# Attention into two expert layers on one core: k and v of two batches loaded as six tokens on 96 partitions, loads ordered apart from their use, half of the sums of squares on VectorE

## The chip, the cores and the metric

The kernel runs on one core of one Trainium2 chip. The metric is the device time of one execution in microseconds (us), lower is better. The kernel before takes 1116.54 us (median of 3 runs, 1115.36 to 1117.87).

## The reference, cut to what matters

All inputs are float32 but for the weights `moe_w1`, `moe_w2`, `moe_w3` and `moe_w_out`, which are float64. `q`, `k` and `v` have the shape (4 batches, 8 heads, 576 tokens, 64).

```
kv  = einsum('bhsd,bhse->bhde', k, v)            # per head: 64 x 64
out = einsum('bhsd,bhde->bhse', q, kv)
rms = sqrt(mean(out*out, axis=-1) + 1e-6)
x   = (out / rms * g_norm), as 2304 tokens x 512
h   = ((x @ moe_w1) * (x @ moe_w2)) @ moe_w3      # d_ff = 1024
y   = h @ moe_w_out                               # 2304 x 512
p   = probs / (sum(probs) + 1e-9)                 # 4 experts
result = sum over e of p[:, e] * (relu(y @ w1[e]) @ w2[e])
```

## The kernel before, in words

**Three stretches.** The attention and the first layer make up the "front" (about the first third of the time). Then three groups of 768 tokens go through the four experts. All large products are done as three matmuls each on parts of the numbers (`mm3`, lines 321 to 325: high x high, high x low, low x high), and many of them in a Winograd-like form with seven products in place of eight. These matmuls on lines 323 to 325 fill TensorE for most of the time.

**The attention, in units.** `unit(b, p)` (line 689) computes two heads of one batch. It loads q, k and v for the first 512 of the 576 tokens, with four tokens on each of 128 partitions (`head_pair`, line 554): 128 x 2 x 256 numbers, 256 KB, in rows of 1 KB. The last 64 tokens of k and v of all eight heads come once for a batch by `rest_kv` (line 563): the tile `kvr`, 64 x 8 x 64 numbers, 128 KB for k and 128 KB for v, in rows of 256 B. On TensorE a unit then has five steps: `outer` (line 713; 8 matmuls of 64 x 64 on `kv` and 2 on `kvr`, into a bank that is copied to `kvb`), the transposes of q (`qs`, line 684, copied to `qt`), `inner` (line 741; `kvb` times `qt`), and, after the norm, the transposes of `x` (line 684). The last 64 tokens of q of two batches together are a `rest_unit` (line 751).

**The norm** (`normed_turned`, line 575). The sum of squares of each head over 64 columns is made in one of two ways. With `summing`, ScalarE squares each of the eight heads by an instruction of its own that also adds up (line 592, 8 ACTIVATEs with an accumulator read behind each). Without, ScalarE squares the whole bank by one instruction (line 588), and VectorE adds up (line 598). In the kernel before, `SUMMING = 18` makes all 18 do it the first way. GpSimd then takes the root (lines 604 and 605), and VectorE scales (line 608). After the transposes, ScalarE or VectorE writes `xr` (line 626) and splits it into `xth` and `xtl` (lines 368 and 373).

**Weights.** `decode` (line 445) loads 512 KB of float64 as `w1raw`, `w2raw`, `woraw` or `w3raw`, and turns them to float32 on ScalarE and VectorE (lines 460 to 494).

**What sets the order.** The program is a list of operations with the engines on which each can run. `FRONT` (line 35) is a list of parts written out by hand; each part is a stage. The planner (`Plan.order`, line 139) walks through time with a cost for each operation, gives each free engine the ready operation of the earliest stage, and writes the instructions in that order. It holds a count of tiles: `RINGS` allows 9 tiles of `attention` (q, k, v) at a time. A load is an operation like the others, queued in its unit's stage. All loads and stores go through one queue, SP's. Eight transfers are under way at a time: the ninth waits until the first has landed, and the two small loads of `g_norm`, which ScalarE issues (line 424), take two of these eight places once. Where TensorE has little to do at the start, `FILL` and `WARM` add matmuls on an identity (lines 420 and 1693), whose results are not used.

Of the kernel before, what the change touches and what calls it, by code (L numbers as in the profile page):

```python
# [13 lines left out]
I64 = mybir.dt.int64  # L14
# [4 lines left out]
P = 128  # L19
RAWS = 5  # L20
TILES = 99
BANKS = 8
RINGS = {"attention": 9, "decoded": 12}
WINDOW = 14
AHEAD = 3
LATER = 6
PLAIN = 1
SUMMING = 18
WARM = 10
# [5 lines left out]
FRONT = (  # L35
# [12 lines left out]
)  # L48
# [210 lines left out]
def attention_moe_kernel(  # L259
# [57 lines left out]
    def half(name, dt=F32, ring=None):  # L317
        return Buf("h", name, [P, 512], dt, ring)
# [23 lines left out]
    def load(buf, *parts, key=None, queue="sp", cost=None):  # L342
        def emit(_):
            for dst, src in parts:
                (nc.sync if queue == "sp" else nc.scalar).dma_start(
                    out=dst(buf.tile), in_=src[:, :] if isinstance(src, Buf) else src
                )

        add(
            {queue: cost or (1.48 if buf.kind == "r" else 0.68)}, emit,  # L350
            reads=[src for _, src in parts if isinstance(src, Buf)], writes=[(buf, key)], latency=2.6,
        )
# [91 lines left out]

    def decode(name, src, shape=None):

# [3 lines left out]

        raw = Buf("r", name + "raw", [P, 512], I64)
        load(raw, ((lambda t: t.rearrange("p (k f) -> p k f", k=KD)) if shape else whole, src))
        val, add_ = half("val", ring="decoded"), half("add", I32, "decoded")
# [118 lines left out]

    summed = []

    def normed_turned(ps, places, whole_values=None):

# [4 lines left out]
        ss = Buf("n", "ss", [P, 8, 1], F32)  # L581

        summing = SUMMING > len(summed)
        summed.append(t)

# [78 lines left out]
    def zeroed(name):  # L664
        t = half(name)
        add({"pool": 0.5}, lambda _: nc.gpsimd.memset(t.tile, 0.0), writes=[t])
        return t
# [20 lines left out]

    def unit(b, p):
        first = b not in kvb  # L690
        if first:
            kvb[b] = zeroed("kvb")
        loaded = []
        for name, src in (("q", q), ("kv", k), ("kv", v)):
            raw = half(name, ring="attention")
            load(raw, (heads, head_pair(src, b, p)), cost=0.82)
            loaded.append(raw)
        qraw, ks, vs = loaded
        if first:
            rest_kv(b)  # L700
        kr, vr = kvr[b]
        ps = bank()

        def outer(e):
# [9 lines left out]

        add({"pe": 0.9}, outer, reads=[ks, vs, kr, vr], writes=[ps])
        for i in range(2):
# [28 lines left out]
        if b == B - 1 and p < HP // 2:  # L745
            normed_turned(po, [], xr[b, p])
        else:
            xt[b, p] = Pair("xt")
            normed_turned(po, [(512, xt[b, p], whole, whole, None)], xr[b, p])

    def rest_unit(g):
        qraw = half("q", ring="attention")
# [26 lines left out]
        if g == 0:  # L779
# [8 lines left out]
            for i in range(2)  # L788
        ])

# [73 lines left out]
    pair_w = {}  # L864
    weights = {}

    def pair_weights(g, n, i):
# [37 lines left out]
        return made  # L905

    def weight(n, f):

        if (n, f) not in weights:
            weights[n, f] = decode(f"w{n + 1}", columns((moe_w1, moe_w2)[n], f), True)  # L910
        return weights[n, f]
# [725 lines left out]
    def expert_shares():  # L1637
# [4 lines left out]
        fn.__name__: fn for fn in (  # L1642
            bilinear_pair, bilinear_plain, expert_shares, mixed, mixed_product,
            norm_scale, rest_unit, row, unit, w3o_summed,
# [33 lines left out]

    for stage, (fn, args) in enumerate(items):
        plan.stage = stage  # L1680
        fn(*args)

    with tc.manual_schedule():
# [42 lines left out]
```

## Time and profile before

| | |
|---|---|
| runs | 1116.54 us median of 3 (1115.36 to 1117.87) |
| profiled execution | 1117.49 us, span 1115.7 us |
| mean granted TensorE clock | 0.998 of full speed |
| TensorE (PE) busy | 1103.3 us, 99% of the span |
| VectorE (DVE) busy | 810.5 us, 73% |
| ScalarE (ACT) busy | 600.6 us, 54% |
| GpSimd (POOL) busy | 47.1 us, 4% |
| DMA | 272.91 MB, 72.5% of the queues' time by SP's queue |

The profiled execution's own time is 1.8 us more than its span (the time from the first to the last instruction), and 0.95 us above the median of the runs. Matmuls are pipelined: one is shown as longer than the distance to the next, so a busy share of 99% alone does not tell how much of it is useful. The trace shows float32 matmuls as two records each (`x8` for the four of line 741).

### The profile page before, as it was taken

The numbers are of one execution on the slowest core, as the hardware profiler recorded it, in microseconds if no ns is written. First come the engines' busy times: TensorE is split into PE (matmuls) and PEld (weight loads), VectorE is DVE, ScalarE is ACT, GpSimd is POOL, SyncE is SP. The second block draws the span as 40 slices with busy tenths as digits, with TensorE's granted clock in tenths as the row PEclk, the third lists the DMA queues.
The fourth block names the chain that finished last, engine by engine and source line by source line (L and its number), as shares of the span: only waits on it lengthen the run. The fifth ranks groups of instructions, "written<-read, shape, count | busy, mean of one in ns | idle before, by whom it ended". The sixth has DMA issues, their size and how long they took to land.

```text
span 1115.7 us, 19375 instructions
## 1 busy us (share of the span) xinstructions
PE 1103.3 (99%) x6856; PEld 1022.3 (92%) x6856; DVE 810.5 (73%) x1656; ACT 600.6 (54%) x1472; POOL 47.1 (4%) x57
## 2 busy tenths in 40 slices
PE   7999999999999999999999999999999999999998
PEld 7888888888888999889999999999999999999998
DVE  4888888889879898788667745547588646474684
ACT  6998754556636655545444455434455445444540
POOL 4513200000000000000000000000000000000000
PEclk9999999999999999999999999999999999999999
DMA  9999993450330599999977935778679867685846
GB/s 272 288 336 329 380 370 102 137 167 20 95 95 29 171 349 351 345 365 327 339 262 239 363 126 198 259 247 288 217 256 328 282 239 259 238 299 195 280 140 203
DMA packets 173697, 272.91 MB, mean 245 GB/s; under 512 B 21792, under 2 KB 89376, under 8 KB 173600
## 3 DMA queue, kind: packets, MB, share of 16 engines
q1 hardware_dynamic: 173440, 271.68, 72.5%
q8 instruction: 54, 0.88, 0.3%
q14 instruction: 43, 0.35, 0.1%
q10 hardware_dynamic: 160, 0.00, 0.0%
HBM read 188.78 MB, written 82.84 MB: 243 GB/s over the span
## 4 chain that ended last, share of the span: by engine, by line
PE 95%; ACT 2%; DMA 1%; DVE 1%; issue 0%; POOL 0%; DVEq 0%; ACTq 0%
PE b L323 30%; PE b L325 30%; PE b L324 30%; PE b L684 2%; PE b L741 1%; PE b L713 1%; DMA q<-in_q_dram 0%; ACT x L592 0%; ACT hth L368 0%; DMA w1raw<-in_moe_w_dram 0%; DMA woraw<-in_moe_w_out_dram 0%; PE b L776 0%; DVE s L1501 0%; DVE acc L1576 0%; ACT qs L729 0%
## 5 line engine op out<-in xcount | busy, mean ns | idle before, releaser
L672 ACT COPY u<-b 128x384 f32<-128x384 f32 (+1 forms) x191 | 96.5, 505 | 194.5 <-PE b L325 189.7
L325 PE MATMUL b<-w,htl 128*128 128x256 f32 x672 | 189.9, 283 | 0.0
L324 PE MATMUL b<-w,hth 128*128 128x256 f32 x672 | 189.8, 282 | 0.0
L323 PE MATMUL b<-w,hth 128*128 128x256 f32 x672 | 189.6, 282 | 0.0
L1401 DVE TENSOR_TENSOR u<-u,b 128x384 f32<-128x384 f32 x144 | 79.5, 552 | 124.2 <-PE b L325 66.9
L1576 DVE SCALAR_TENSOR_TENSOR acc<-b,pn,acc 128x256 f32<-128x256 f32 x144 | 68.7, 481 | 85.1 <-PE b L325 84.9
L325 PEld LDWEIGHTS b<-w,htl 128*128 128x128 f32 x672 | 128.4, 191 | 0.0
L323 PEld LDWEIGHTS b<-w,hth 128*128 128x128 f32 x672 | 128.0, 191 | 0.2
L324 PEld LDWEIGHTS b<-w,hth 128*128 128x128 f32 x672 | 128.1, 191 | 0.0
L368 ACT CAST hth<-s 128x384 fp32r<-128x384 f32 x128 | 62.9, 512 | 51.1 <-DVE s L1501 48.0
L1412 ACT ACTIVATE u<-u 128x384 f32<-128x384 f32 x96 | 50.5, 526 | 62.0 <-DVE u L1401 61.9
L325 PE MATMUL b<-wdh,htl 128*128 128x512 f32 x192 | 75.5, 393 | 0.0
L324 PE MATMUL b<-wdl,hth 128*128 128x512 f32 x192 | 75.4, 393 | 0.0
L323 PE MATMUL b<-wdh,hth 128*128 128x512 f32 x192 | 74.7, 389 | 0.0
L373 DVE TENSOR_TENSOR htl<-s,hth 128x384 fp32r<-128x384 f32 x128 | 67.3, 550 | 3.5 <-ACT hth L368 3.5
L373 DVE TENSOR_TENSOR htl<-u,hth 128x384 fp32r<-128x384 f32 x96 | 49.9, 551 | 5.8 <-ACT hth L368 5.8
L368 ACT CAST hth<-u 128x384 fp32r<-128x384 f32 x96 | 46.3, 510 | 0.4
L323 PE MATMUL b<-th,weh 128*128 128x512 f32 x112 | 44.5, 397 | 0.4 <-ACT u L672 0.4
L325 PE MATMUL b<-th,wel 128*128 128x512 f32 x112 | 43.7, 390 | 0.0
L324 PE MATMUL b<-tl,weh 128*128 128x512 f32 x112 | 43.7, 390 | 0.0
L325 PEld LDWEIGHTS b<-wdh,htl 128*128 128x128 f32 x192 | 36.0, 188 | 7.6
L324 PEld LDWEIGHTS b<-wdl,hth 128*128 128x128 f32 x192 | 36.0, 188 | 5.9
(291 smaller groups left out, 3037.8 us busy)
## 6 DMA issues: line engine op xcount, KB each, us to landing
we<-we SPq DMA_DIRECT2D x240, 256.0 KB, 5.3
w<-w2kept SPq DMA_DIRECT2D x112, 512.0 KB, 4.5
we<-weh SPq DMA_DIRECT2D x48, 256.0 KB, 3.8
we<-wel SPq DMA_DIRECT2D x48, 256.0 KB, 3.7
w3raw<-in_moe_w_dram SPq DMA_DIRECT2D x16, 512.0 KB, 3.7
e1raw<-in_moe_w_dram SPq DMA_DIRECT2D x32, 256.0 KB, 4.4
e2raw<-in_moe_w_dram SPq DMA_DIRECT2D x32, 256.0 KB, 4.4
w2kept<-wth SPq DMA_DIRECT2D x32, 256.0 KB, 3.8
```

What stands on the lines that cost most here:

```text
L323: nc.tensor.matmul(ps, w[0], x[0], start=first, stop=False, skip_group_check=more)
L324: nc.tensor.matmul(ps, w[0], x[1], start=False, stop=False, skip_group_check=more)
L325: nc.tensor.matmul(ps, w[1], x[0], start=False, stop=last, skip_group_check=more)
L368: nc.scalar.copy(to(dst.high.tile), value(src.tile))
L373: nc.vector.tensor_tensor(out=to(dst.low.tile), in0=value(src.tile), in1=to(dst.high.tile), op=ALU.subtract)
L672: lambda e: nc.scalar.copy(to(dst.tile), value(src.tile)) if e == "act"
L684: nc.tensor.transpose(ps[:, c], raw[:, c], ident)
L713: nc.tensor.matmul(ps[c, c], a, b_, start=r == 0, stop=r == R)
L741: nc.tensor.matmul(po[:, c], qt[:, c], kvb[b][:, p * P:(p + 1) * P], start=True, stop=True)
L1401: lambda _: nc.vector.tensor_tensor(out=t[:, :W], in0=base[:, :W], in1=ps[:, :W], op=ALU.add),
L1412: lambda eng: nc.scalar.activation(out=t[:, :W], in_=src[:, :W], func=ACTF.Relu)
L1576: nc.vector.scalar_tensor_tensor(out=a[:, to], in0=ps[:, c], scalar=sc, in1=a[:, to], op0=ALU.mult, op1=ALU.add)
```

## The change

**Loads of k and v.** For batches 0 and 1 (`SIXES`) k and v of a unit are loaded head by head: all 576 tokens as six on each of 96 partitions, four loads of 96 x 384 numbers (144 KB, rows of 1.5 KB) in place of two of 256 KB. `outer_sixes` has 12 matmuls of 64 x 64 on 96 rows in place of 10. The `kvr` tiles of these two batches, their loads and their zeroing on GpSimd fall away. Batches 2 and 3 are as before.

**Loads as parts.** `fetch` and `fetch_weight` are parts of `FRONT` of their own, ahead of the unit or weight that uses them, and don't count as a stage. `FRONT` is a new list, the ring of attention tiles is 12 in place of 9.

**Sums of squares.** Each unit has a third number, `summing`. Nine of 18 have 1 (ScalarE adds up, as before); nine have 0 (one square of 128x512 on ScalarE, the sum on VectorE).

```diff
-RINGS = {"attention": 9, "decoded": 12}
+RINGS = {"attention": 12, "decoded": 12}
...
+SIXES = (0, 1)
 PLAIN = 1
-SUMMING = 18
...
 FRONT = (
...
+    "norm_scale, fetch 1 2, fetch_weight 1 4, fetch_weight 0 7, unit 1 2 0, fetch 1 3, weight 1 4, "
+    "fetch_weight 1 0, fetch 1 1, weight 0 7, fetch 1 0, unit 1 3 0, unit 1 0 0, fetch 0 0, fetch 0 1, "
+    "fetch 0 2, fetch_weight 0 3, fetch 0 3, unit 1 1 0, unit 0 0 0, unit 0 1 1, unit 0 2 1, weight 1 0, "
+    "fetch 3 1, unit 0 3 0, bilinear_plain 0 0, rest_unit 0 1, unit 3 1 0, fetch 2 0, weight 0 3, unit 2 "
+    "2 1, unit 2 0 1, bilinear_plain 1 0, bilinear_pair 0 3, unit 2 1 1, bilinear_pair 0 2, unit 3 2 0, "
+    "unit 3 0 0, unit 3 3 1, bilinear_pair 0 1, unit 2 3 1, rest_unit 1 1, bilinear_pair 1 2, "
...
-    def normed_turned(ps, places, whole_values=None):
+    def normed_turned(ps, places, whole_values=None, summing=0):
...
+    def fetch(b, p):
+        loaded = fetched[b, p] = []
         for name, src in (("q", q), ("kv", k), ("kv", v)):
+            if b in SIXES and name == "kv":
+                for h in range(2):
+                    raw = half(name, ring="attention")
+                    load(raw, (
+                        lambda t: t[0:96, 0:6 * D].rearrange("p (r d) -> p r d", r=6),
+                        src[b, 2 * p + h].rearrange("(p r) d -> p r d", r=6),
+                    ), cost=0.45)
+                    loaded.append(raw)
+                continue
             raw = half(name, ring="attention")
             load(raw, (heads, head_pair(src, b, p)), cost=0.82)
             loaded.append(raw)
...
+            def outer_sixes(e):
+                for r in range(6):
+                    for h in range(2):
+                        c, m = slice(h * D, (h + 1) * D), slice(r * D, (r + 1) * D)
+                        nc.tensor.matmul(
+                            ps[c, c], kvs[h][0:96, m], kvs[2 + h][0:96, m], start=r == 0, stop=r == 5
+                        )
...
+    def fetch_weight(n, f):
+        weights_raw[n, f] = fetch_raw(f"w{n + 1}", columns((moe_w1, moe_w2)[n], f), True)
...
-    for stage, (fn, args) in enumerate(items):
-        plan.stage = stage
+    for fn, args in items:
         fn(*args)
+        plan.stage += fn not in (fetch, fetch_weight)
```

What this does to the order of the instructions is shown for three engines. The first is SP, the queue of the loads, from the first instruction of the program. Before:

```order
L345 DMA w1raw<-in_moe_w_dram 128x4x128
L345 DMA q<-in_q_dram 128x2x256
L345 DMA kv<-in_k_dram 128x2x256
L345 DMA kv<-in_v_dram 128x2x256
L345 DMA kvr<-in_k_dram 64x8x64
L345 DMA kvr<-in_v_dram 64x8x64
L345 DMA q<-in_q_dram 128x2x256
L345 DMA kv<-in_k_dram 128x2x256
L345 DMA kv<-in_v_dram 128x2x256
```

The same place of SP's queue now (line 346 is line 345 of the kernel before):

```order
L346 DMA q<-in_q_dram 128x2x256
L346 DMA kv<-in_k_dram 96x384 x2
L346 DMA kv<-in_v_dram 96x384 x2
L346 DMA w2raw<-in_moe_w_dram 128x4x128
L346 DMA w1raw<-in_moe_w_dram 128x4x128
L346 DMA q<-in_q_dram 128x2x256
L346 DMA kv<-in_k_dram 96x384 x2
L346 DMA kv<-in_v_dram 96x384 x2
L346 DMA w2raw<-in_moe_w_dram 128x4x128
```

The first unit's q, k and v stand ahead of all weights, and no load of `kvr` stands between the first eight units any more; up to the eighth unit there are four loads of weights (three before).

The second is TensorE (PE) around the first matmul of the bilinear layer (`xth`, `wh`; lines 323 to 325), behind the eighth unit's `outer`. Before:

```order
L684 MATMUL b<-ident,x 128x128 x4
L741 MATMUL b<-kvb,qt 128x128 x4
L713 MATMUL b<-kv 64x64 x8
L713 MATMUL b<-kvr 64x64 x2
L741 MATMUL b<-kvb,qt 128x128 x4
L684 MATMUL b<-ident,qs 128x128 x4
L323 MATMUL b<-xth,wh 128x512
L324 MATMUL b<-xtl,wh 128x512
L325 MATMUL b<-xth,wl 128x512
```

The same place now (722 is `outer_sixes`, 771 is `inner`, 324 to 326 is `mm3`):

```order
L684 MATMUL b<-ident,x 128x128 x4
L771 MATMUL b<-kvb,qt 128x128 x4
L722 MATMUL b<-kv 64x64 x12
L771 MATMUL b<-kvb,qt 128x128 x4
L684 MATMUL b<-ident,qs 128x128 x4
L324 MATMUL b<-xth,wh 128x512
L325 MATMUL b<-xtl,wh 128x512
L326 MATMUL b<-xth,wl 128x512
```

In both programs TensorE has done the same steps of units ahead of this matmul: eight times `outer`, seven times `inner`, eight transposes of q and four of `x`; each `outer` now has 12 matmuls in place of 10, and 12 fill matmuls stand among them in place of 20.

The third is ScalarE (ACT), from the first unit's copy of `qs`. Before:

```order
L729 COPY qs<-q 128x2x4x64
L672 COPY qt<-b 128x512
L368 CAST weh<-val 128x512
L729 COPY qs<-q 128x2x4x64
L672 COPY kvb<-b 64x64 x2
L672 COPY qt<-b 128x512
L592 ACTIVATE x,ss<-b 128x64 x8
L672 COPY kvb<-b 64x64 x2
```

The same place of ScalarE now:

```order
L759 COPY qs<-q 128x2x4x64
L672 COPY qt<-b 128x512
L672 COPY kvb<-b 64x64 x2
L465 ACTIVATE val<-w2raw 128x512
L474 ACTIVATE add<-w2raw 128x512
L465 ACTIVATE val<-w1raw 128x512
L588 ACTIVATE x<-b 128x512
L759 COPY qs<-q 128x2x4x64
```

The first unit's eight squares with sums (line 592) are one square of the whole bank (line 588); the sum is a TENSOR_REDUCE on VectorE (line 598).

## Rows read from the trace of the kernel before

**Rows 1.** The page's part 1: busy us (share of the span) and instructions of each engine.

```profile
PE 1103.3 (99%) x6856; PEld 1022.3 (92%) x6856; DVE 810.5 (73%) x1656; ACT 600.6 (54%) x1472; POOL 47.1 (4%) x57
```

**Rows 2.** Waits of PE from 37.3 us on: us in total, times, longest.

```profile
PE b L323 <- ACT u L672: 1.3, 5, 0.4
```

**Rows 3.** Chain of waits that ended last: start us, us, what.

```profile
15.10 1.35 PE b L741 x8
16.47 1.75 ACT x L592 x16
...
39.34 0.73 PE b L713 x20
...
43.44 0.44 PE b L684 x4
46.64 0.89 PE b L741 x8
```

**Rows 4.** Timeline of PE: start us, us, instruction [idle before <- releaser].

```profile
8.56 0.69 PE L713 MATMUL b<-kv 128*64 128x64 f32 x16 [0.90 <-DMA kv<-in_v_dram]
10.80 0.34 PE L713 MATMUL b<-kvr 128*64 128x64 f32 x4 [1.55 <-DMA kvr<-in_v_dram]
...
37.27 0.48 PE L323 MATMUL b<-xth,wh 128*128 128x512 f32 x1
...
38.05 0.40 PE L323 MATMUL b<-xth,wh 128*128 128x512 f32 x1
38.28 0.39 PE L324 MATMUL b<-xtl,wh 128*128 128x512 f32 x1
```

**Rows 5.** Stretches: length, busy us by engine, granted PE clock, DMA share, GB/s.

```profile
0.00:10.00 10.00, 7.01 (x52) 6.71 (x52) 0.96 (x4) 3.81 (x6) 6.73 (x19) 1.00 0.84 203
10.00:18.00 8.00, 6.27 (x54) 5.86 (x54) 4.85 (x9) 3.57 (x21) 0.00 (x0) 0.79 1.09 348
...
20.00:22.00 2.00, 2.00 (x32) 1.80 (x30) 1.51 (x4) 1.98 (x18) 0.39 (x1) 1.00 1.25 248
22.00:24.00 2.00, 1.40 (x26) 1.15 (x25) 1.33 (x2) 1.95 (x7) 1.72 (x2) 1.00 1.15 191
```

**Rows 6.** Timeline of SP's queue: start us, us, the load that is issued.

```profile
0.72 0.46 SPq L345 DMA_DIRECT2D w1raw<-in_moe_w_dram  x1
1.24 0.49 SPq L345 DMA_DIRECT2D q<-in_q_dram  x1
...
2.80 0.75 SPq L345 DMA_DIRECT2D kvr<-in_k_dram  x1
...
7.20 0.37 SPq L345 DMA_DIRECT2D kv<-in_k_dram  x1
...
15.74 0.37 SPq L345 DMA_DIRECT2D kv<-in_k_dram  x1
...
29.55 0.37 SPq L345 DMA_DIRECT2D kv<-in_v_dram  x1
```

**Rows 7.** Waits of all engines up to 37.3 us: the one of `g_norm`.

```profile
DVE g L425 <- DMA graw<-in_g_norm_dram: 9.0, 1, 9.0
```

**Rows 8.** Groups of ACT up to 45 us: xcount | busy us, mean ns | idle before.

```profile
L592 ACT ACTIVATE x<-b 128x64 f32<-128x64 f32 x64 | 13.3, 248 | 2.2 <-PE b L741 2.2
...
L729 ACT COPY qs<-q 128x512 f32<-128x512 f32 x6 | 3.7, 617 | 0.0
...
L672 ACT COPY qt<-b 128x512 f32<-128x512 f32 x5 | 3.0, 597 | 1.7 <-PE b L684 1.6
```

**Rows 9.** Groups of DVE up to 45 us, columns as in rows 8.

```profile
L608 DVE TENSOR_TENSOR x<-b,ss 128x512 f32<-128x512 f32 x7 | 4.8, 692 | 2.1 <-POOL ss L605 1.9
...
L474 DVE TENSOR_SCALAR val<-val 128x512 f32<-128x512 f32 x3 | 1.3, 421 | 0.0
```

**Rows 10.** Stretches, columns as in rows 5: a dip of the clock, a later stretch.

```profile
12.00:16.00 4.00, 3.29 (x16) 3.29 (x17) 2.35 (x5) 1.55 (x5) 0.00 (x0) 0.57 1.09 348
...
75.00:150.00 75.00, 75.00 (x462) 63.44 (x461) 66.88 (x126) 60.41 (x208) 14.99 (x14) 1.00 1.02 356
```

More of the change, by code (lines that the diff above doesn't have):

```diff
@@ L442, in shares, with fetch_raw, decode @@
         nc.vector.tensor_tensor(out=pn, in0=praw, in1=prec.to_broadcast([P, NT // P, NE]), op=ALU.mult)
-    def decode(name, src, shape=None):
+    def fetch_raw(name, src, shape):
         raw = Buf("r", name + "raw", [P, 512], I64)
         load(raw, ((lambda t: t.rearrange("p (k f) -> p k f", k=KD)) if shape else whole, src))
+        return raw
+    def decode(name, src, shape=None, raw=None):
+        raw = fetch_raw(name, src, shape) if raw is None else raw
         val, add_ = half("val", ring="decoded"), half("add", I32, "decoded")
@@ L571, in rest_kv @@
             )
-    summed = []
-    def normed_turned(ps, places, whole_values=None):
+    def normed_turned(ps, places, whole_values=None, summing=0):
         t = half("x")
         ss = Buf("n", "ss", [P, 8, 1], F32)
-        summing = SUMMING > len(summed)
-        summed.append(t)
         def square(e):
@@ L687, in turned @@
         return ps
[L689 to L693, printed above, removed]
-        for name, src in (("q", q), ("kv", k), ("kv", v)):
+    fetched = {}
+    def fetch(b, p):
+        loaded = fetched[b, p] = []
+        for name, src in (("q", q), ("kv", k), ("kv", v)):
+            if b in SIXES and name == "kv":
[7 more added lines that the diff above has]
+                continue
             raw = half(name, ring="attention")
@@ L697, in unit @@
             loaded.append(raw)
[L698 to L701, printed above, removed]
-        ps = bank()
+    def unit(b, p, summing=0):
+        if b not in kvb:
+            kvb[b] = zeroed("kvb")
+        sixes = b in SIXES
+        if (b, p) not in fetched:
+            fetch(b, p)
+        loaded = fetched[b, p]
+        ps = bank()
+        if sixes:
+            qraw, *kvs = loaded
+            def outer_sixes(e):
[5 more added lines that the diff above has]
+                        )
+            add({"pe": 1.08}, outer_sixes, reads=kvs, writes=[ps])
+        else:
+            qraw, ks, vs = loaded
+            if b not in kvr:
+                rest_kv(b)
+            kr, vr = kvr[b]
         def outer(e):
@@ L713, in outer @@
                     nc.tensor.matmul(ps[c, c], a, b_, start=r == 0, stop=r == R)
-        add({"pe": 0.9}, outer, reads=[ks, vs, kr, vr], writes=[ps])
+        if not sixes:
+            add({"pe": 0.9}, outer, reads=[ks, vs, kr, vr], writes=[ps])
         for i in range(2):
@@ L745, in unit, with rest_unit @@
         if b == B - 1 and p < HP // 2:
-            normed_turned(po, [], xr[b, p])
+            normed_turned(po, [], xr[b, p], summing)
         else:
             xt[b, p] = Pair("xt")
-            normed_turned(po, [(512, xt[b, p], whole, whole, None)], xr[b, p])
-    def rest_unit(g):
+            normed_turned(po, [(512, xt[b, p], whole, whole, None)], xr[b, p], summing)
+    def rest_unit(g, summing=0):
         qraw = half("q", ring="attention")
@@ L788, in rest_unit @@
             for i in range(2)
-        ])
+        ], summing=summing)
     def x_of(xs, b, kk):
@@ L865, in attention_moe_kernel @@
     weights = {}
+    weights_raw = {}
     def pair_weights(g, n, i):
@@ L905, in pair_weights @@
         return made
+    def fetch_weight(n, f):
+        weights_raw[n, f] = fetch_raw(f"w{n + 1}", columns((moe_w1, moe_w2)[n], f), True)
     def weight(n, f):
         if (n, f) not in weights:
-            weights[n, f] = decode(f"w{n + 1}", columns((moe_w1, moe_w2)[n], f), True)
+            if (n, f) not in weights_raw:
+                fetch_weight(n, f)
+            weights[n, f] = decode(f"w{n + 1}", None, True, weights_raw[n, f])
         return weights[n, f]
@@ L1642, in attention_moe_kernel @@
         fn.__name__: fn for fn in (
-            bilinear_pair, bilinear_plain, expert_shares, mixed, mixed_product,
+            bilinear_pair, bilinear_plain, expert_shares, fetch, fetch_weight, mixed, mixed_product,
             norm_scale, rest_unit, row, unit, w3o_summed,
```

19 rows, old and new, of the table FRONT are left out of this document.

## The prediction

> **What bounds the kernel now.** I read the page's busy shares first: TensorE is busy for 1103.3 of 1115.7 us [rows 1], so only work of TensorE that falls away, or time in which it waits, can be gained. The view of its waits comes next: from 37.3 us to the end it waits 1.3 us in all, in five pieces [rows 2]. Everything behind that time is bound by TensorE's own work, which the change leaves almost as it is. So the change is decided in the first 37 us. There the timeline shows TensorE waiting for loads (0.90 us for v, 1.55 us for the small rows of `kvr` [rows 4]), and the chain of waits runs through the squares on ScalarE, 1.75 us each [rows 3].
>
> How much of the 37.3 us is useful can be counted. The first matmul of the bilinear layer starts at 37.27 us [rows 4]. Ahead of it TensorE has done eight `outer` at 0.73 us, seven `inner` at 0.89 us and twelve groups of transposes at 0.44 us [rows 3]: 5.8 + 6.2 + 5.3 = 17.3 us. The other 20 us are warm-up, fill and waits. The new program does the same steps ahead of its first such matmul, so its start against 37.27 us is the gain, as long as TensorE doesn't have to wait again later.
>
> **The change part by part.** *TensorE.* Eight `outer` have 12 matmuls in place of 10: 0.73 x 12 / 10 = 0.88 us, 0.15 us more each, 1.2 us in all. The trace has no matmul on 96 rows; the nearest are these same 64-column ones on 128 rows, and I take their price (below: 0.73, nothing more; above: 12 matmuls at half clock, 1.75). All eight lie ahead of the first bilinear matmul, so that 1.2 us lies beside the loads. The eight fills fewer cost nothing: TensorE was waiting anyway.
>
> *Loads.* This is where I expect the new end of the start. A pair of `kvr` loads has 0.26 MB, but rows of 256 B: while the second pair was under way the rate fell from 348 to 248 and 191 GB/s [rows 5], which loses 2 x (100 + 157) KB = 0.51 MB, or 1.5 us at 348 GB/s; with its own 0.75 us a pair takes 2.2 us or more. Two pairs leave the start. Up to the eighth unit's last v the new queue has 8 q of 0.262 MB, 32 six-token loads of 0.147 MB and four weights of 0.524 MB: 8.91 MB. In the first 10 us 203 GB/s were moved, 2.03 MB [rows 5]; without `kvr` in that stretch I allow up to 2.4 MB. The rest at 348 GB/s takes 18.7 to 19.8 us, so the bytes are through at 28.7 to 29.8 us. A landing comes later than that: the load issued at 15.74 us [rows 6] had waited for the one eight places ahead, whose bytes (3.41 MB from the start) are through at 10 + (3.41 - 2.03) / 0.348 = 14.0 us by the same count. So 1.8 us more: the eighth unit lands at 30.5 to 31.6 us, I take 31.0. Behind it `outer` (0.88), `inner` (0.89) and the transposes of q (0.44) follow on TensorE: the first bilinear matmul at **33.2 us**.
>
> For the price of a six-token load the trace has no row. By bytes it is 0.147 / 0.348 = 0.42 us; no less than SP's issue of 0.37 us [rows 6] below, no more than a load of 128 x 2 x 256, 0.75 us, above. I take 0.42, since its rows of 1.5 KB are nearer to those of 1 KB that ran at 348 GB/s than to those of 256 B. The Trainium skill (DMA: Bandwidth & Descriptors, Why a DMA increments its semaphore by 16 and not by 1) says that a tile of 96 partitions is spread over 16 engines as one of 128 is. No run here shows that yet; by it the price would be the 0.42 us taken, and by an uneven spread it would be nearer to 0.75.
>
> *ScalarE and VectorE.* Up to that point ScalarE had seven squares of 1.75 us [rows 3], 12.3 us. Now there are five plain ones on the path to the first bilinear matmul; a square of 128x512 out of PSUM is not in the trace, the nearest are the copies `qt` and `qs` of that size, 0.60 and 0.62 us [rows 8] (below 0.25, one of the eight small ones [rows 8]; above 1.75): 3.0 us. So 9.3 us leave ScalarE, which would end about 28 us if nothing else held it. VectorE gets the five sums at the price of the scaling of the same size, 0.69 us [rows 9] (below 0.42, the fast form; above twice 0.69). It still starts at 9.0 us, as `g_norm` lands then [rows 7]; ahead of the first bilinear matmul it has 23 operations of 0.69 and 12 of 0.42 us [rows 9]: 20.9 us, done at 29.9 us without a gap. So DMA is last, VectorE 2 to 3 us ahead of it: those two are late next.
>
> *SP's queue.* The load behind the first eight still waits for `g_norm`: in the trace the one at 7.20 us [rows 6] did. The first unit's q is issued at 0.72 in place of 1.24 us [rows 6], ahead of all weights; the second unit's k and v stay behind `g_norm`. The larger ring (12) adds no wait.
>
> *Behind 33.2 us.* The rest of q (0.26 MB in rows of 256 B) and the `kvr` of batch 3 now come behind three loads of 0.262 MB and two weights, 1.84 MB or 5.3 us after the eighth unit: 36.3 us, then 2.2 us for each pair, so 38.5 and 40.7 us. TensorE needs them after 18 matmuls at 0.23 us [rows 4], two transposes and one `inner`: 33.2 + 4.1 + 0.9 + 0.9 = 39.1 us, and some 2.9 us later. That is tight; I put 0.3 us there (between 0 and 2.6).
>
> *The sum.* 33.2 - 37.27 + 0.3 = -3.8 us. Against the profiled execution's 1117.49 us that is 1113.7; this execution lies 0.95 us above the median of the runs, so against 1116.54 I forecast **1112.7 us**. A difference of 0.2% (2.2 us) is about what a measurement of this kernel can tell from none.
>
> **The rivals.** *The six-token loads are slow (slower).* If one takes as long as a load of 128 x 2 x 256, the start gets 32 x 0.33 = 10.6 us later than taken: the first bilinear matmul at 43.8 us, in all 1123 us. It turns at 0.42 + 4.1 / 32 = 0.55 us for each. For it: twice as many loads in SP's queue, each with an issue and one of only eight places, and an issue of 0.37 to 0.75 us [rows 6]. Against: rows of 1.5 KB, and loads of a third fewer rows than 128. Chance 0.12.
>
> *The time is given back later.* Between 75 and 150 us VectorE is busy for 66.9 of 75 us and the queue is full [rows 10]. If what VectorE and the loads deliver there comes no earlier than before, TensorE starts sooner and waits sooner: 1116.5 us. For it: the share, and a new order of all weights. Against: TensorE didn't wait there once [rows 2], ScalarE and VectorE have less or as much to do, and 4.4 us of loads are gone. Chance 0.16.
>
> *The clock.* From 12 to 16 us TensorE had 0.57 of its clock, that is mostly the lower level of 1.2 GHz, after waits of 0.90 and 1.55 us [rows 4, 10]; `inner` took 1.35 us in place of 0.89 [rows 3]. With fewer fills and waits for each unit's loads, such a stretch may return and stay. The steps between 12 and 30 us are some 15 us; half of them at half clock adds 7.5 us, of which the waits hide some 5: 2.5 us later, 1115.2 us. Chance 0.12. The Trainium skill (TensorE: Matmul & The Clock Gate, Loop structure matters more than you think) names a wait for DMA between matmuls as what lets the engine go cold. By that rule the time comes out as in this rival; the row of 12 to 16 us agrees with it.
>
> **How the numbers follow.** The forecast has 0.60, the rivals 0.12, 0.16 and 0.12. Faster by over 0.2%: 0.58 of the forecast, 0.07 of the clock, 0.01 of the slow loads (only a little slow): 0.66. Slower: 0.09 of the slow loads and 0.03 of the time given back: 0.12. The same: 0.22. The range takes in a start that VectorE alone bounds (29.9 + 0.7 us, 1109.8) and reaches up to the time given back with a small loss: 1109.5 to 1117.2 us; outside lie the slow loads and a little below.
>
> **What would show it.** Right: the first bilinear matmul near 33 us, no `kvr` wait ahead of it, TensorE's waits behind it under 2 us, a square near 0.6 us, six-token loads issued every 0.4 to 0.5 us. Wrong: TensorE waiting for `kv` with the queue's rate well under 340 GB/s, a clock under 1 from 16 to 30 us, or new waits for `kvr`, `wl` or `xtl` behind 33 us.

## The result, and the profile of the changed kernel

| | before | changed |
|---|---|---|
| median of the runs (us) | 1117.01 (1115.36 to 1118.26, 6 runs) | 1123.82 (1122.21 to 1125.51, 6 runs) |
| profiled execution (us) | 1117.49 | 1122.78 |
| its span (us) | 1115.7 | 1121.0 |
| first bilinear matmul (us) | 37.27 | 42.33 |

The ratio is 1.0057, with a 95% interval of 1.0046 to 1.0068: the change makes the kernel slower by some 6.4 us (0.0057 x 1117; the medians lie 6.8 us apart), where 3.8 us of gain were forecast. It lies outside the range. The time is that of the first rival, the slow six-token loads (1123 us, first bilinear matmul at 43.8 us), which had a chance of 0.12.

The page's part 1, then the waits of TensorE over the whole span (engine and line, what it waited for: us in total, times, longest us):

```profile
PE 1105.6 (99%) x6872; PEld 1025.2 (91%) x6872; DVE 809.9 (72%) x1652; ACT 599.8 (54%) x1350; POOL 46.2 (4%) x53
```

```profile
PE b L684 <- ACT qs L759: 4.6, 2, 4.2
PE b L722 <- DMA kv<-in_v_dram: 2.7, 3, 2.2
...
PE b L324 <- ACT u L672: 1.0, 4, 0.3
```

The line on `u` is all that stands behind the first bilinear matmul. It answers to [rows 2] with 1.0 in place of 1.3 us, so nothing is lost there: from the first bilinear matmul to the end of the span it is 1121.0 - 42.33 = 1078.7 us, before it was 1115.7 - 37.27 = 1078.4. The work ahead of it is also the same, eight `outer`, seven `inner` and twelve groups of transposes. All that the change costs lies in the first 42 us.

The timeline of TensorE there (start us, us, instruction [idle before <- releaser]; answers to [rows 4]):

```profile
14.41 1.11 PE L684 MATMUL b<-ident,qs 128*128 128x128 f32 x4 [4.16 <-ACT qs L759]
15.82 2.03 PE L722 MATMUL b<-kv 96*64 96x64 f32 x24 [0.30 <-DMA kv<-in_v_dram]
...
23.01 0.92 PE L722 MATMUL b<-kv 96*64 96x64 f32 x24
...
35.84 1.98 PE L722 MATMUL b<-kv 96*64 96x64 f32 x24 [2.17 <-DMA kv<-in_v_dram]
...
40.13 0.92 PE L722 MATMUL b<-kv 96*64 96x64 f32 x24
...
42.33 0.48 PE L324 MATMUL b<-xth,wh 128*128 128x512 f32 x1
```

Two gaps stand out: 4.16 us for the second unit's `qs`, and 2.17 us for the seventh unit's v at 35.84 us. Behind each gap the same `outer` takes 2.0 us in place of 0.92. The stretches tell why, and how the loads go (length, busy us by engine, granted PE clock, DMA share, GB/s; they answer to [rows 5, 10]):

```profile
0.00:10.00 10.00, 8.65 (x74) 8.47 (x74) 0.15 (x1) 3.10 (x6) 4.04 (x14) 1.00 0.63 191
10.00:20.00 10.00, 4.95 (x38) 4.05 (x37) 6.70 (x13) 5.75 (x12) 2.93 (x2) 0.62 1.12 246
20.00:30.00 10.00, 9.30 (x119) 8.52 (x117) 5.61 (x10) 8.39 (x20) 5.03 (x7) 0.87 0.97 256
...
14.00:22.00 8.00, 6.70 (x45) 5.99 (x46) 5.52 (x11) 4.92 (x10) 2.93 (x2) 0.50 1.11 241
...
36.00:38.00 2.00, 1.86 (x25) 1.60 (x25) 0.63 (x3) 0.14 (x1) 0.63 (x1) 0.56 1.07 285
```

From 14 to 22 us the granted clock is 0.50, the level of 1.2 GHz, and behind the second gap it falls again, to 0.56 from 36 to 38 us. And from 10 to 20 us the queue moves 246 GB/s where the kernel before moved 348 [rows 5, 10], although the share of the DMA engines is higher (1.12 against 1.09): the engines aren't short of work, each byte takes longer. The chain of waits (start us, us, what) runs through these loads, and the queue of SP (start us, us, issue; answers to [rows 6]) issues the eighth unit's v at 31.67 to 33.20 us, when by the forecast it had landed:

```profile
13.73 6.96 DMA kv<-in_k_dram
...
24.96 4.25 DMA kv<-in_k_dram
29.23 7.01 DMA kv<-in_v_dram
36.28 1.54 PE b L722 x22
```

```profile
0.72 0.45 SPq L346 DMA_DIRECT2D q<-in_q_dram  x1
1.23 0.92 SPq L346 DMA_DIRECT2D kv<-in_k_dram  x2
...
6.60 0.90 SPq L346 DMA_DIRECT2D kv<-in_k_dram  x2
...
31.67 1.53 SPq L346 DMA_DIRECT2D kv<-in_v_dram  x2
```

### The profile page after: what moved, and what is told of

Same layout as the page of the kernel before. It is cut to its first block, busy times and chain, and to the rows that moved or that the text cites. A ratio compares the mean times of both kernels' runs of the same rounds, so it can differ in the third digit from the quotient of the medians.

```text
span 1121.0 us, 19295 instructions
## 1 busy us (share of the span) xinstructions
PE 1105.6 (99%) x6872; PEld 1025.2 (91%) x6872; DVE 809.9 (72%) x1652; ACT 599.8 (54%) x1350; POOL 46.2 (4%) x53
## 4 chain that ended last, share of the span: by engine, by line
PE 95%; DMA 3%; DVE 1%; ACT 1%; SPq 0%; issue 0%; ACTq 0%; DVEq 0%
PE b L324 31%; PE b L326 30%; PE b L325 30%; PE b L684 2%; DMA q<-in_q_dram 1%; DMA kv<-in_k_dram 1%; PE b L771 1%; DMA kv<-in_v_dram 1%; PE b L742 1%; SPq L346 0%; ACT hth L369 0%; PE b L806 0%; DVE s L1537 0%; PE b L722 0%; DVE acc L1612 0%
## 5 line engine op out<-in xcount | busy, mean ns | idle before, releaser
L988 DVE TENSOR_TENSOR u<-u,b 128x512 f32<-128x512 f32 x42 | 28.7, 686 | 19.4 <-PE b L326 12.1
```

The lines of the kernel that those rows point to most:

```text
L988: lambda _: nc.vector.tensor_tensor(out=t.tile, in0=t.tile, in1=ps.tile, op=ALU.add),
```

## The experiments

The table has all runs. Each ratio is to the kernel before, run beside it, with its 95% interval; the start is the first bilinear matmul in the profile; rate and share are those of the stretch from 10 to 20 us. In most runs the same steps of units lie ahead of the start as in the changed kernel or as many. The exceptions: e2 has a ninth `outer` and one group of transposes more, e7, e12 and e13 one group of transposes more, e14 one `inner` fewer, e11 one `inner` and one group of transposes fewer. e4, e9, e10, e12 and e13 leave k^T v of batches 0 and 1 uncomputed or take it from part of the tokens: they show times, and aren't variants to use.

| run | what it is | time (us) | ratio | start (us) | GB/s, share |
|---|---|---|---|---|---|
| e1 | new order, four-token loads | 1117.45 | 1.0004 (0.9995 to 1.0013) | 37.16 | 348, 1.09 |
| e2 | old order, six-token loads | 1124.12 | 1.0064 (1.0042 to 1.0087) | 43.96 | 240, 0.98 |
| e3 | the sums alone | 1118.71 | 1.0017 (1.0005 to 1.0030) | 35.66 | 348, 1.09 |
| e4 | 128 rows of 1152 bytes | 1117.87 | 1.0009 (0.9998 to 1.0020) | 36.20 | 313, 1.01 |
| e5 | changed, with fills | 1123.66 | 1.0069 (1.0046 to 1.0091) | 41.42 | 266, 1.11 |
| e6 | second head on 32 to 127 | 1164.18 | 1.0415 (1.0396 to 1.0433) | 82.10 | 270, 1.13 |
| e7 | e6, mended order | 1168.74 | 1.0451 (1.0418 to 1.0485) | 86.25 | 274, 0.95 |
| e8 | e1, mended order | 1117.69 | 1.0006 (0.9996 to 1.0016) | 36.41 | 320, 0.99 |
| e9 | 128 rows of 1536 bytes | 1120.86 | 1.0031 (1.0015 to 1.0046) | 39.52 | 348, 1.04 |
| e10 | 96 rows of 1024 bytes | 1118.49 | 1.0014 (1.0004 to 1.0025) | 38.14 | 212, 0.88 |
| e11 | nine tokens on 128 rows | 1125.02 | 1.0072 (1.0055 to 1.0089) | 40.08 | 369, 1.06 |
| e12 | e4, mended order | 1121.59 | 1.0037 (1.0022 to 1.0051) | 41.15 | 314, 1.00 |
| e13 | e4, second unit first | 1117.81 | 1.0001 (0.9991 to 1.0011) | 36.03 | 326, 1.03 |
| e14 | e1, second unit first | 1117.97 | 1.0005 (0.9996 to 1.0015) | 34.63 | 349, 1.09 |

### Which part costs the time: e1, e2, e3

The theories: the six-token loads move slowly (S), or the new order of steps does it (O). e1 takes the loads back and leaves the rest of the change:

```diff
-SIXES = (0, 1)
+SIXES = ()
...
+        if b < 2 and b not in SIXES and b not in kvr:
+            rest_kv(b)
```

> The changed kernel with the four-token loads and kvr of batches 0 and 1 put back; the new order of steps and the new split of the squares' sums stay. Theory S (the six-token loads move their bytes slower: 225 to 300 GB/s in the changed kernel against 348 before): between 10 and 20 us the queue moves 330 GB/s or more, the first bilinear matmul starts at 37 us or earlier (42.33 in the changed kernel), time 1118 us or less. Theory O (the new order puts the second unit's loads behind two weights and its qs copy behind two decodes on ScalarE): TensorE still idles about 4 us near 10 to 14 us, its clock is 0.50 for some microseconds behind that, the first bilinear matmul starts at 40 us or later, time 1121 to 1124 us.

e2 is the reverse: the table of the kernel before, every sum on ScalarE, and the six-token loads (the ring stays at 12).

```diff
-    "norm_scale, fetch 1 2, fetch_weight 1 4, fetch_weight 0 7, unit 1 2 0, ...
+    "norm_scale, weight 0 7, unit 1 3 1, unit 1 2 1, weight 1 4, weight 1 0, ...
```

> The six-token loads alone, in the order of steps of the kernel before, with all the squares' sums on ScalarE as before. Theory S: the queue moves 240 to 300 GB/s between 10 and 30 us, the first bilinear matmul at 41 to 44 us, time 1120 to 1125 us. Theory O: no idle stretch of 4 us, the queue is faster than in the changed kernel, the first bilinear matmul at 37.5 us or earlier, time 1117 us or less.

e3 has the sums alone: that table with the last argument of `unit` and `rest_unit` as in the change, `SIXES = ()`, and the ring of 9.

> The new split of the squares' sums alone: loads, kvr and the order of steps as in the kernel before. Both theories say that this part does no harm: first bilinear matmul at 35 to 37.3 us, time 1114 to 1117 us. If VectorE is the one that is late with nine sums more, the first bilinear matmul comes later than 38 us, or new waits appear between 75 and 150 us, and the time is 1118 us or more.

The stretch from 10 to 20 us of e1, then that of e2:

```profile
10.00:20.00 10.00, 5.75 (x41) 5.04 (x41) 6.55 (x13) 7.40 (x14) 2.67 (x2) 0.65 1.09 348
```

```profile
10.00:20.00 10.00, 6.24 (x64) 5.67 (x63) 3.51 (x8) 6.56 (x39) 1.91 (x2) 0.88 0.98 240
```

S holds at both ends: without these loads the rate is back at 348 GB/s and the time is that of the kernel before (the start of 37.16 us lies just over the 37 that S had named); with them alone the kernel loses as much as the whole change does. O falls as the cause of the loss. Still e1 has its idle stretch (3.7 us for `qs`) and a clock of 0.65, and with both it is no slower than before. In e14, below, the idle stretch is gone and the start comes 2.5 us earlier, some 0.9 us of it by one `inner` fewer ahead, but the time stays the same.

e3 starts 1.6 us earlier than the kernel before and still is 0.17% slower, at 1118.71 us where 1114 to 1117 were expected. In its trace the stretch behind the start takes 1116.0 - 35.66 = 1080.3 us, 1.9 us more than before. TensorE waits 0.8 us for `kvr` and v there; the rest of the difference isn't explained.

### Which property of the loads: e4, e9, e10, e6

Four runs vary the shape. e4 has the same bytes and the same count on all partitions, e9 the same rows of 1536 bytes on all partitions (a third more bytes), e10 the 96 partitions with short rows (a third fewer bytes), e6 the same loads with every second one at the other end of the partitions.

```diff
-lambda t: t[0:96, 0:6 * D]...     src[b, 2 * p + h].rearrange("(p r) d -> p r d", r=6)
+lambda t: t[:, 0:288]             (e4: the head's 36864 floats as 128 rows)
+lambda t: t[:, 0:384]             (e9: 49152 floats from the head's start as 128 rows)
+lambda t: t[0:96, 0:256]          (e10: the head's first 24576 floats as 96 rows)
+lambda t: t[32 * h:32 * h + 96, 0:6 * D]...                     (e6: rows as before)
```

> The changed kernel, but each k or v of a head in batches 0 and 1 is loaded as 128 rows of 288 floats (1152 bytes) in place of 96 rows of 384 floats: the same bytes, the same number of loads, all 128 partitions. The six matmuls of a head read columns 0 to 287 of it, so k^T v of batches 0 and 1 isn't computed (the pairs of k and v rows aren't whole tokens); all else is. If the loads are slow because of their 96 partitions: 330 GB/s or more between 10 and 20 us, the first bilinear matmul at 37 us or earlier, 1118 us or less. If they are slow because there are more of them and each is small (eight places, an issue for each), or if order and clock are what counts: 225 to 300 GB/s as in the changed kernel, the first bilinear matmul at 41 us or later, 1121 to 1125 us.

> The changed kernel, but each k or v of a head in batches 0 and 1 is loaded as 128 rows of 384 floats: the changed kernel's rows of 1536 bytes, all 128 partitions, a third more bytes (the rows aren't whole tokens, and k^T v of these batches isn't computed). Read as the busy share of the 16 DMA engines for each 100 GB/s between 10 and 20 us: 0.31 in the kernel before (1.09 at 348), 0.46 in the changed kernel (1.12 at 246). If the 96 partitions are what is slow: 0.34 or less. If rows of 1536 bytes are: 0.43 or more, and the first bilinear matmul at 45 us or later. By the bytes alone (32 x 49 KB more, 4.5 us at 348 GB/s) it starts near 40.5 us.

> The changed kernel, but each of these loads is 96 rows of 256 floats (1024 bytes) on 96 partitions: two thirds of the bytes, the rows as long as in the kernel before (a third of the tokens is left out of k^T v of batches 0 and 1). If the 96 partitions are what is slow: the share for each 100 GB/s between 10 and 20 us stays at 0.40 or more. If rows of 1536 bytes are: 0.34 or less, and the queue runs short of loads rather than of engines.

> The changed kernel, but the six-token loads of the second head of each unit go to partitions 32 to 127 in place of 0 to 95 (two matmuls, of 32 and 64 rows, for each token of that head: 18 in place of 12 in an outer). Same bytes, rows of the same 1536 bytes, 96 partitions in each load, the same number of loads. Theory P (the partitions 0 to 63 take the bytes of a load more slowly than the rest can make up: by 96 of them the lower 64 get two thirds of the bytes, on half of the ways into SBUF): with the two heads on opposite ends the rate comes back to 310 GB/s or more between 10 and 20 us, the first bilinear matmul at 38 us or earlier, time 1119 us or less. Rival (each small load, or its rows of 1.5 KB, or a spread over fewer DMA engines is slow): 240 to 260 GB/s, the first bilinear matmul at 42 us or later, 1123 to 1126 us.

The start of e4 and of e9 in the timeline of TensorE:

```profile
36.20 0.48 PE L324 MATMUL b<-xth,wh 128*128 128x512 f32 x1
```

```profile
39.52 0.48 PE L324 MATMUL b<-xth,wh 128*128 128x512 f32 x1
```

The stretch from 10 to 20 us of e4, e9, e10 and e6, in this order:

```profile
10.00:20.00 10.00, 6.44 (x51) 5.73 (x50) 7.47 (x15) 7.38 (x14) 2.94 (x2) 0.66 1.01 313
```

```profile
10.00:20.00 10.00, 7.22 (x74) 6.50 (x75) 6.57 (x13) 6.72 (x15) 2.93 (x2) 0.79 1.04 348
```

```profile
10.00:20.00 10.00, 6.30 (x46) 5.64 (x45) 7.12 (x15) 6.48 (x13) 2.96 (x3) 0.61 0.88 212
```

```profile
10.00:20.00 10.00, 8.81 (x52) 6.78 (x51) 5.07 (x11) 4.43 (x9) 2.94 (x2) 0.67 1.13 270
```

The share for each 100 GB/s is 0.32 in e4 and 0.30 in e9, on 128 partitions; it is 0.42 in e10 and 0.42 in e6, on 96, and 0.46 in the changed kernel (0.41 in e2, 0.42 in e5). Only e7 has less, 0.35; weights of 512 KB are issued there at 6.0, 7.3 and 14.3 us, and from 20 to 30 us it has 0.44 too (1.11 at 255 GB/s). e4's rate of 313 GB/s stays under the 330 that were expected, e10's queue also runs short of loads (share 0.88). So the length of the rows isn't it, nor the count of loads, nor SP's issues: the 96 partitions are. The plainest pair is e9 against the changed kernel: 1.57 MB more to load, and the start comes 2.8 us earlier (39.52 against 42.33 us).

The packets of these traces (the pieces in which a load is moved), counted from 10 to 20 us, say it more directly. One of 1536 bytes takes 112 ns on average in the changed kernel and 71 ns in e9. One of 1024 bytes, which comes from loads of 128 partitions alone, takes 72 ns in the changed kernel and 50 ns in e9, and 51 ns in the kernel before. So the six-token loads slow the loads beside them as well.

Why 96 partitions cost more stays open. The theory behind e6 fell: with the heads on opposite ends the rate came to 270 GB/s, not to 310, and e5 below, whose loads are those of the changed kernel, has 266 GB/s at the same 0.42. The Trainium skill (SBUF — State Buffer, Door 1: The DMA port swizzle) says that partitions 0 to 63 share half of the ways into SBUF; by that, 96 partitions would run at three quarters of the rate, 261 GB/s, as an estimate from the 348 of the trace. The 240 to 266 GB/s of the changed kernel, e2 and e5 lie near it, but e6, which evens the load out, doesn't bear it out as the whole reason.

e6 is also 40 us slower, for a reason on TensorE. The first `outer` in its timeline, 18 matmuls of 96, 32 and 64 rows in turn:

```profile
8.06 4.67 PE L723 MATMUL b<-kv 96*64 96x64 f32 x36
```

That is 4.67 us in place of 0.92, and later ones take up to 7.32, at the half clock. So e6 tells of the rate between 10 and 20 us, and nothing of the start.

### What the half clock costs: e5

```diff
-FILL = {1: 3, 2: 3, 3: 2}
+FILL = {1: 3, 4: 6, 5: 3}
```

> The changed kernel with more fill matmuls (six ahead of each group of the second unit, three ahead of the third's) in place of the idle stretch near 10 to 14 us: it tests what the half clock behind that stretch costs. Theory C (clock): the granted clock from 14 to 22 us stays near 1.00 in place of 0.50, the first bilinear matmul comes 3 us or more earlier than 42.33, time 1121 us or less. Theory P (the 96-partition loads bound the start): whatever the clock, the last loads land at the same time, the first bilinear matmul stays at 41 us or later, time 1122.5 to 1125 us.

The stretch of 14 to 22 us of e5, and its first bilinear matmul in the timeline of TensorE:

```profile
14.00:22.00 8.00, 8.00 (x102) 7.53 (x100) 5.96 (x11) 5.18 (x10) 4.27 (x4) 1.00 1.08 263
```

```profile
41.42 0.48 PE L324 MATMUL b<-xth,wh 128*128 128x512 f32 x1
```

With fills in the gap the clock is 1.00 there, and from 36 to 40 us too, where the changed kernel fell a second time. The start gains 0.9 us, the time nothing that can be measured (1123.66 against 1123.82 us). The half clock was there, mostly beside the loads that set the end. The fills cost something of their own, though: from 20 to 30 us the queue of e5 moves 225 GB/s where the changed kernel moves 256, so 0.9 us may not be the whole of what the half clock takes.

### Would the rest of the forecast have held: e7, e8, e12, e13, e14

With full-rate loads e4 still starts at 36.20 us, 3 us behind the 33.2 of the forecast, and has 3.0 us of idle near 10 us. The "mended order" tries to close that gap: the second unit ahead of the two weights, `g_norm` loaded behind the first `qt`, and the fills moved to the first two units (`FILL = {0: 3, 1: 3, 2: 2}`).

```diff
-    "norm_scale, fetch 1 2, fetch_weight 1 4, fetch_weight 0 7, unit 1 2 0, fetch 1 3, weight 1 4, ...
+    "fetch 1 2, fetch 1 3, fetch_weight 1 4, fetch_weight 0 7, unit 1 2 0, fetch 1 1, unit 1 3 0, ...
+        if (b, p) == (1, 2):
+            add({"act": 1.4}, load_norm, reads=[qt], writes=[xscale], latency=2.5)
```

> As the run with the second head on partitions 32 to 127, and beside it the second unit's loads and steps ahead of the two weights, g_norm loaded behind the first unit's qt (so that no load of SP's queue waits for it), and the fills of the first two units kept. Theory P plus O (with the full rate back, the idle stretch of 3 to 4 us near 10 to 14 us is what is left of the loss): no wait above 2 us of TensorE there, the first bilinear matmul at 32.5 to 35 us, time 1113 to 1116 us. If the order doesn't matter, because the loads' last bytes set the end: the first bilinear matmul at 36 to 38 us, time 1117 to 1119 us.

> The four-token loads with kvr of batches 0 and 1, and the same mended order: second unit ahead of the weights, g_norm behind the first qt. Against the run with four-token loads in the order of the change (1117.45 us, 37.16 us to the first bilinear matmul, 3.7 us of idle near 10 to 14 us). If that idle stretch sets the end: 34 to 35.5 us, time 1114.5 to 1116 us. If the bytes set it: 36.5 to 37.5 us, time 1116.5 to 1118 us.

> The loads of 128 rows of 288 floats (k^T v of batches 0 and 1 isn't computed, as in the run with these loads before), and beside them the mended order: the second unit's loads and steps ahead of the two weights, g_norm loaded behind the first unit's qt, the fills of the first two units kept. With these loads alone the first bilinear matmul came at 36.20 us, with 3.0 us of idle near 10 to 13 us and a granted clock of 0.66 from 10 to 20 us. Theory (the forecast of 33.2 us missed two things: the rate of the 96-partition loads, and the idle stretch that the new order itself makes): 32.5 to 34.5 us, clock 1.00 from 10 to 20 us, 1113.5 to 1116 us. If a third thing bounds the start (VectorE's or ScalarE's own work, or the bytes at less than 348 GB/s): 35 us or later, 1116.5 to 1118.5 us.

e7 carries e6's slow `outer` and tells nothing more. e8 came out at 36.41 us and 1117.69 us, close to what was expected if the bytes set the end: TensorE waits 2.9 us for v there. e12 missed, by a wait that the edit itself brought in: the scaling of `g_norm` stands first in VectorE's order. VectorE's waits of e12 up to 20 us:

```profile
DVE g L426 <- DMA graw<-in_g_norm_dram: 14.0, 1, 14.0
```

It did nothing for 14.0 us, where it was 9.0 before [rows 7], and the second unit's `qs` stood behind that wait in e12. e13 and e14 leave `norm_scale` first and move only the second unit ahead of the weights:

```diff
-    "norm_scale, fetch 1 2, fetch_weight 1 4, fetch_weight 0 7, unit 1 2 0, fetch 1 3, weight 1 4, ...
+    "norm_scale, fetch 1 2, fetch 1 3, fetch_weight 1 4, fetch_weight 0 7, unit 1 2 0, unit 1 3 0, ...
```

> The loads of 128 rows of 288 floats once more (k^T v of batches 0 and 1 isn't computed), and of the order only this is changed: the second unit's loads and steps stand ahead of the two weights and their decoding; g_norm stays first. (The run before this one had moved g_norm too, and VectorE then waited for it ahead of the second unit's qs.) If the forecast's 33.2 us would have come true with the full rate but for the idle stretch that the new order makes: no wait of TensorE over 2 us near 10 to 14 us, the first bilinear matmul at 32.5 to 35 us (36.20 without this edit), time 1113.5 to 1116.5 us. If something else bounds the start (the decoding of the weights on VectorE, ScalarE's order, the last loads): 35.5 us or later, 1117 us or more.

> The same change of order with the four-token loads and kvr of batches 0 and 1 (a whole, correct variant of the change without its loads; 37.16 us to the first bilinear matmul and 1117.45 us without this edit). If the idle stretch near 10 to 14 us bounds it: 34 to 36 us, time 1114.5 to 1116.5 us, faster than the kernel before. If the bytes with two pairs of kvr bound it: 36.5 to 38 us, 1117 to 1118.5 us.

The stretches of e13, and its timeline of TensorE at the end of the start:

```profile
10.00:20.00 10.00, 8.39 (x98) 7.18 (x97) 6.64 (x13) 8.23 (x18) 4.90 (x6) 1.00 1.03 326
20.00:30.00 10.00, 9.91 (x147) 8.91 (x146) 7.82 (x14) 8.94 (x21) 4.66 (x6) 1.00 1.06 330
```

```profile
32.43 1.33 PE L722 MATMUL b<-kv 128*64 128x64 f32 x24 [0.82 <-DMA kv<-in_v_dram]
33.88 1.16 PE L771 MATMUL b<-kvb,qt 128*128 128x128 f32 x8
34.88 0.60 PE L684 MATMUL b<-ident,x 128*128 128x128 f32 x4
35.62 0.66 PE L684 MATMUL b<-ident,qs 128*128 128x128 f32 x4
36.03 0.48 PE L324 MATMUL b<-xth,wh 128*128 128x512 f32 x1
```

The gap is gone and the clock is 1.00, and the start is still at 36.03 us, with one group of transposes more ahead of it than in e4. So the gap took less than 1 us of it. The last v lands at 32.4 us (31.0 in the forecast), and 3.6 us of steps follow it (2.2 in the forecast). In e14 the start came at 34.63 us, with one `inner` fewer ahead of it, and the time stayed that of the kernel before (1114.5 to 1116.5 us were expected): behind the start its profile takes 1115.6 - 34.63 = 1081.0 us, 2.5 us more than that of the kernel before. One `inner` of 0.9 us stands there now, and TensorE waits 1.9 us for `u` where it waited 1.3; the rest wasn't taken apart. No variant here beats the kernel before.

### All 128 partitions with whole tokens: e11

```diff
-TILES = 99
+TILES = 93
...
+raw = Buf("k", "kv", [P, 576], F32)
+src[b, 2 * p:2 * p + 2].rearrange("h (p r) d -> (h p) r d", r=9)
+for h in range(2):
+    for r in range(9):
+        nc.tensor.matmul(ps[c, c], k9[c, m], v9[c, m], start=r == 0, stop=r == 8)
```

> The same aim as the change on all 128 partitions: nine tokens on each of 64 partitions, head 0 on 0 to 63 and head 1 on 64 to 127, so that one load of 128 rows of 2304 bytes brings k (or v) of both heads whole, without kvr; 18 matmuls of 64 rows an outer, those of head 0 first. Tiles of 576 columns need room: 93 in place of 99 tiles for the rest. If the 96 partitions are what is slow: 330 GB/s or more between 10 and 20 us, the last loads as early as predicted for the change; what is left is the idle stretch of 3 to 4 us and its half clock: first bilinear matmul at 34 to 37 us, time 1113.5 to 1118 us. If small pieces on TensorE are slow as in the run with 32 and 64 rows (there an outer took 4.7 us and more): the first bilinear matmul at 45 us or later, 1125 us or more.

The rate is 369 GB/s from 10 to 20 us, the best of all runs. But an `outer` of 18 matmuls of 64 rows costs TensorE 2.13 us; the first one in the timeline, and the stretch from 20 to 30 us:

```profile
8.15 2.13 PE L722 MATMUL b<-kv 64*64 64x64 f32 x36
```

```profile
20.00:30.00 10.00, 10.00 (x149) 9.58 (x149) 6.20 (x12) 6.90 (x16) 6.28 (x9) 1.00 0.70 222
```

TensorE is busy for all 10 us and the queue runs short of loads (share 0.70): between 18 and 30 us SP waits 7.5 us for `outer` on TensorE, until one of the six tiles of 576 columns is free. Eight of them cost 8 x (2.13 - 0.92) = 9.7 us more. The bound moved from the loads to TensorE, and the time is no better than that of the change (ratio 1.0072 against 1.0057, with intervals that overlap). The start of 40.08 us lies between the two that were expected.

## Why the prediction was wrong

- **What bounds the kernel.** Right: the change was decided ahead of the first bilinear matmul, and behind it all stayed as it was.
- **The price of a six-token load** is the step that failed. It was taken as 0.147 / 0.348 = 0.42 us, "since its rows of 1.5 KB are nearer to those of 1 KB that ran at 348 GB/s". The row was chosen by the length of rows, and e9 and e10 show that this counts little and the number of partitions much. At the rate of the changed kernel the load takes 0.147 / 0.246 = 0.60 us. Against e4 (same bytes, same count, same work ahead) the start is 42.33 - 36.20 = 6.13 us later, 0.19 us for each of 32 loads; e4's own load is 0.147 / 0.313 = 0.47 us, which makes 0.66 us, with the slower loads beside it and the half clock from 36 us on counted in. So a six-token load costs 0.60 to 0.66 us, an estimate from these rows. That is inside the bounds (0.37 to 0.75) and beyond the point at which the first rival was to decide (0.55). The upper bound, the load of 128 x 2 x 256, came nearer to the result (a start of 43.8 us). The shape of the forecast's sum was right: with the measured 246 GB/s and 1.91 MB in the first 10 us it gives 10 + (8.91 - 1.91) / 0.246 + 1.8 + 2.2 = 42.5 us, where 42.33 was measured. Some luck is in that nearness: from 20 us on the rate was 256 GB/s and more, and the half clock from 36 to 40 us made up for it.
- **The Trainium skill's spread over 16 engines** (DMA: Bandwidth & Descriptors, Why a DMA increments its semaphore by 16 and not by 1): the mean share of 1.12 is as high as with 128 partitions and gives no sign of idle engines, but it doesn't show the engines one by one. It didn't follow that the price is 0.42 us.
- **Bytes of the first 10 us.** Up to 2.4 MB were allowed, 1.91 came (191 GB/s, share 0.63 in place of 0.84 [rows 5]). This term was too large too, by 0.49 / 0.348 = 1.4 us. In the same order e1, with four-token loads, moved 2.23 MB and e4, with small loads on 128 partitions, 2.05; that eight small loads under way hold fewer bytes is a likely reason, and not shown.
- **`outer`.** Right: 0.92 us in the record, where 0.88 was worked out from [rows 3]. At half clock two of them took 2.0 us, over the bound of 1.75. Most of it lay beside the loads.
- **Squares and sums.** The prices were right. The groups of ScalarE and VectorE up to 45 us (xcount | busy us, mean ns | idle before):

```profile
L588 ACT ACTIVATE x<-b 128x512 f32<-128x512 f32 x5 | 3.0, 597 | 0.3 <-PE b L771 0.2
```

```profile
L598 DVE TENSOR_REDUCE ss<-x 128x8 f32<-128x512 f32 x5 | 3.4, 683 | 2.4 <-ACT x L588 2.4
```

  0.60 and 0.68 us, as put (0.69 for the sum). In the changed kernel what left ScalarE left no path that set the end; in e3, without the six-token loads, the start came 1.6 us earlier with the sums alone.
- **The end of the start at full rate.** e13 shows 36.0 us in place of 33.2. The last v came 1.4 us later than forecast, at a rate of 326 to 330 and not 348 GB/s and with 2.03 MB in the first 10 us. Behind it 1.4 us are added: a fourth step, the transposes of `x` (0.7 us to the next step), and an `outer` that takes 1.45 us to the next step in place of 0.88. So even with loads of the same size on all partitions the gain would have been near nothing: e4 and e13 are within 0.1% of the kernel before.
- **The rivals.** Slow loads: right in place and direction. Its price of 0.75 us was above the 0.60 to 0.66 worked out here; that its time (1123 us) came so near is in part luck, since it left out the bytes of the first 10 us and the half clock. Given back later: wrong for the change, the stretch behind the start is 1078.7 us against 1078.4. Where a variant did start early it came true in part: that stretch is 1080.2 us in e4 (TensorE waits 0.8 us for the rest of q there), 1080.3 in e3 and 1081.0 in e14. The clock: the half clock came, after a wait of 4.16 us for `qs` and again after one of 2.17 us for v. The Trainium skill (TensorE: Matmul & The Clock Gate, Loop structure matters more than you think) names a wait for DMA between matmuls as what lets the engine go cold; the second wait is of that kind, the first is not. Without the half clock e5 starts 0.9 us earlier, since the loads end late; the 2.5 us put for it are not reached there.

## What to carry to other kernels

A load's price follows its shape in partitions as well as its bytes: where no row of the trace has the shape, take the bound that the nearest load *in shape* gives, and try one such load before moving 32 of them. A load of 128 partitions with more bytes can be the faster one. When a start is bound by its last loads, idle engines, a half clock or cheaper squares ahead of them cost little (0.9 us for the half clock in e5) until the loads come earlier.

## What the runs showed of the hardware

- With loads of 96 partitions among the others the DMA engines had a share of 0.41 to 0.46 for each 100 GB/s from 10 to 20 us (the changed kernel, e2, e5, e6, e10), with loads of 128 partitions alone 0.30 to 0.32 (e4, e9), at rows of 1 to 1.5 KB alike. Half of the loads on partitions 32 to 127 (e6) had 0.42, as e5 had without that.
- Beside loads of 96 partitions those of 128 partitions moved more slowly too: 72 ns for a packet of 1024 bytes in the changed kernel, 50 ns in e9.
- Matmuls that change between 96 rows, 32 rows and 64 rows at other partitions are slow: 18 of them took 4.67 us (e6, at a granted clock of 1.00), while 18 of 64 rows, nine at a time on the same partitions, took 2.13 us (e11) and 12 of 96 rows 0.92 us.
